# Sigmoid attention followed by a gated FFN on one core: one FFN chunk between the last score units of batch 0, one pair of loads ahead of two weight loads, one DMA transpose sooner

## The chip, the cores and the metric

The kernel runs on one core of one Trainium2 chip. The metric is device microseconds (us) of one execution; the number compared is the median over runs. A profiled execution gives the trace that is read here. Times written like 49.38 are microseconds from the start of that execution's span.

## The reference

Two layers follow each other. `q`, `k` and `v` have 8 batches, 12 heads, 448 rows and head size 64.

```python
scores = q @ k.transpose(0, 1, 3, 2) / np.sqrt(64) - np.log(448)
attn = 1.0 / (1.0 + np.exp(-scores))
x = (attn @ v).transpose(0, 2, 1, 3).reshape(3584, 768)
gate = np.maximum(x @ w_gate, 0.0)        # 768 x 1536
val = x @ w_val                           # 768 x 1536
out = (gate * val) @ w_out                # 1536 x 768
```

The sigmoid has no row sum, so a score block can be turned into attention values as soon as it is computed. All inputs and the output are float32; the kernel computes matmuls in float16 with float32 sums.

## The kernel before

The heads of a batch are worked off in three groups of four heads (`g` = 0 to 2). The scores of a group need its queries and keys transposed: `qkT`. For batches 0 and 1 TensorE does that (`pe_transposes`, L195: fourteen transposes each for keys and queries into a PSUM bank, then one VectorE copy into `qkT`, L206). From batch 2 on, `dma_transposes` (L211) does it: two VectorE copies put keys and queries into a buffer `rel` (L215; two such buffers take turns), and a DMA transpose issued by SyncE writes `qkT` (three buffers).

The steps that follow are:

- A **score unit** multiplies one 64-column chunk of keys with the queries (`qk`, L232, matmuls of 64x64 tiles, four running in the four quarters of the array), and ScalarE writes the sigmoid into `PT` (L187).
- **pv** (L250) multiplies `PT` with the values, and VectorE scales the result into `xT` (L184), the FFN's input.
- An **FFN chunk** (`gv`, L304) is six matmuls with a 128-column block `f` of `w_gate` and six with that of `w_val` (both L309), then a relu and a product into `hT` (L327). The relu is on VectorE (L320) for the first four chunks and on ScalarE (L318) for the next ones. The chunks wait in `gv_queue` in a fixed order, and `ffn_mix(n)` takes n of them.
- The down projection with `w_out` comes later, and from batch 2 on the matmuls use a scheme with fewer products (L393). The change does not touch that part.

The order on every engine is the order in which the program is written out. For batch 0 it is a list of six **slots** (three groups, first 256 queries and then the other 192), each of four units. A dictionary `after` says what follows unit `u` of slot `i`. The slots' score banks are two pairs of PSUM banks used in turn, so a unit waits until the sigmoid of the unit two before has read its pair; four other banks serve transposes, pv and FFN chunks in rotation. Around the change the list reads:

```python
(4, 1): lambda: ffn_then_pv(3),
(4, 3): lambda: ffn_mix(2),
(5, 1): slots[4].pv,
(5, 2): lambda: (pe_transposes(1, 0, 0), pe_transposes(1, 0, 1)),
```

After the last unit comes `slots[5].pv()`, and then batch 1 starts with group 0, whose `qkT` the transposes at (5, 2) make. Batches 1 to 7 run in **bursts** of score units with FFN chunks between them. Batch 1 has six bursts with 4, 3, 3, 3, 3, 4 chunks; `hooks` puts other work between a burst's chunks: an entry `(n, job)` runs when n chunks of that burst are left. `both(1, 1)` and `both(1, 2)` are TensorE transposes of batch 1's second and third group; `dma_transposes(2, 0)`, `(2, 1)` and `late_loads` belong to batch 2. `late_loads` (L741) does `dma_transposes(2, 2)`, then `hold(2, 2)`, a GpSimd copy that waits for that transpose, then the loads of batch 2's values and of `w_out`, in that order on GpSimd's queue.

All loads but the first two are issued by GpSimd into one DMA queue, in the order of the program, as float32 in memory and float16 on the chip. An issue waits until the load eight places before it has landed. `load(b, g0, g1, "kq")` issues keys and then queries of a batch's group (L110, 224 KB each as written), `load_gv(f0, f1)` issues the blocks f0 to f1 - 1 of `w_gate` and then of `w_val` (L148, 576 KB each for three blocks). Twenty FFN chunks of batch 0 run in batch 1; the first that needs block 9 is the first chunk of the fifth burst.

Of the kernel before, what the change touches and what calls it, by code (L numbers as in the profile page):

```python
# [17 lines left out]
def kernel(  # L18
# [62 lines left out]
    def bank16(name):  # L81
        return bank(name, (P, 1024), FP16)
# [11 lines left out]
    def tiles_of(b):  # L94
        if b not in in_tiles:
            pool = early if b == 1 else inp
            in_tiles[b] = tuple(
                p.tile([P, NPAIR, NCH * D], FP16, tag=t, name=t)
                for p, t in ((pool, "k16"), (pool, "q16"), (vinp, "v16"))
            )  # L100
        return in_tiles[b]

    def rows_of(src, b):
        return src[b].rearrange("(x r) (t c) d -> (r t) x (c d)", r=2, c=NCH)

    def load(b, g0, g1, which, c0=0, c1=NCH):
        for nm, t16, src in zip("kq", tiles_of(b), (k, q)):
            if nm in which:
                xs, cs = slice(2 * g0, 2 * g1), slice(c0 * D, c1 * D)
                nc.gpsimd.dma_start(t16[:, xs, cs], rows_of(src, b)[:, xs, cs])  # L110

    def load_v(b):
        v16 = tiles_of(b)[2]
        nc.gpsimd.dma_start(v16[:, 0::2, :], rows_of(v, b)[:, 0::2, :])
        for r in range(2):
            nc.gpsimd.dma_start(
                v16[64 - 64 * r : P - 64 * r, 1::2, :], rows_of(v, b)[64 * r : 64 * r + 64, 1::2, :]
            )
# [25 lines left out]
    def load_gv(f0, f1, which=(0, 1)):  # L144
        fs = slice(f0 * P, f1 * P)
        for i in which:
            wt, src = ((wg, moe_w_gate), (wv, moe_w_val))[i]
            nc.gpsimd.dma_start(wt[:, :, fs], src[:, fs].rearrange("(c p) f -> p c f", p=P))  # L148
# [7 lines left out]
    load_gv(6, 9)  # L156
    load(1, 1, 2, "kq")
    load_v(1)
    load_gv(9, 12)
    load(1, 2, 3, "kq")  # L160

    def load_o():
        for m0, m1 in ((0, 512), (512, DM)):
# [26 lines left out]
    def qkT_of(b, g):  # L190
        if (b, g) not in qkT_tiles:
            qkT_tiles[(b, g)] = qkTp.tile([P, TW, P], FP16, tag="qkT", name="qkT")
        return qkT_tiles[(b, g)]

    def pe_transposes(b, g, ti, c0=0, c1=NCH):  # L195
        t16 = in_tiles[b][ti]
        qkT = qkT_of(b, g)
        trt = bank16("trt")
        for c in range(c0, c1):
            for h in range(2):  # L200
                nc.tensor.transpose(
                    trt[64 * h : 64 * h + 64, c * P : (c + 1) * P],
                    t16[:, 2 * g + h, c * D : (c + 1) * D],
                    ident[:],
                )
        nc.vector.tensor_copy(  # L206
            qkT[:, ti * NCH + c0 : ti * NCH + c1, :].rearrange("p c x -> p (c x)"),
            trt[:, c0 * P : c1 * P],
        )

    def dma_transposes(b, g):  # L211
        k16, q16, _ = in_tiles[b]
        rel = relp.tile([P, TW, P], FP16, tag="rel", name="rel")
        for ti, t16 in enumerate((k16, q16)):
            nc.vector.tensor_copy(  # L215
                rel[:, ti * NCH : (ti + 1) * NCH, :].rearrange("p c (h d) -> p h c d", h=2),
                t16[:, 2 * g : 2 * g + 2, :].rearrange("p h (c d) -> p h c d", c=NCH),
            )
        nc.sync.dma_start_transpose(
            qkT_of(b, g)[:], rel[:].rearrange("p c x -> p (c x)")  # L220
        )
# [437 lines left out]
    def ffn_mix(count, hooks=()):  # L659
        hooks = list(hooks)  # L660
        for left in range(count, -1, -1):
            while hooks and hooks[0][0] >= left:
                hooks.pop(0)[1]()
            if left:
                gv_queue.popleft()()
# [10 lines left out]
    slots = [FirstSlot(half * NG + g, g, half) for half in range(2) for g in range(NG)]  # L676
# [5 lines left out]
    def first_of_second_group():  # L682
        pe_transposes(0, 1, 0, 0, KCUT)
        pe_transposes(0, 1, 1, 0, QCUT)

    def ffn_then_pv(i):
        ffn_mix(1)
        slots[i].pv()
# [16 lines left out]
        (3, 2): second_queries,  # L705
        (3, 3): lambda: ffn_mix(1),
        (4, 1): lambda: ffn_then_pv(3),
        (4, 3): lambda: ffn_mix(2),
        (5, 1): slots[4].pv,
        (5, 2): lambda: (pe_transposes(1, 0, 0), pe_transposes(1, 0, 1)),  # L710
    }
    for i, slot in enumerate(slots):
        for u in range(4):
# [23 lines left out]
    def both(b, g):  # L737
        pe_transposes(b, g, 0)
        pe_transposes(b, g, 1)
# [49 lines left out]
    for b in range(1, B):  # L789
        if b == 1:  # L790
            cuts, pv_at = (0, 3, 6, 9, 13, 17, 21), {3: (0, 2), 5: (1, 2)}
        else:
            cuts, pv_at = (0, 4, 7, 11, 14, 18, 21), {0: (-1, 2), 2: (0, 2), 4: (1, 2)}
        bursts = list(range(len(cuts) - 1))
        inner = {}
        if b > 2:
            inner = {0: 1} if b % 2 == 0 else {2: 3, 3: 5} if b == B - 1 else {4: 5}
            for n in inner.values():
                bursts.remove(n)
        count = len(bursts)  # L800
        hooks = {}
        if b == 1:
            mix = (4, 3, 3, 3, 3, 4)
            hooks = {
                1: [(1, lambda: both(1, 1))],
                3: [(1, lambda: both(1, 2))],
                4: [(3, lambda: dma_transposes(2, 0)), (1, lambda: dma_transposes(2, 1))],
                5: [(3, late_loads)],
            }
        elif b == 2:  # L810
            mix = (2, 2, 1, 1, 1, 2)
            hooks = {
                2: [(0, prepare)],
                4: [(0, lambda: weight_sums(0))],
                5: [(1, lambda: weight_sums(1)), (0, lambda: weight_sums(2))],
            }
            open_late()
        elif b == 3:
            mix = (1, 1, 1, 0, 0)
        else:  # L820
            mix = (0,) * count

        def burst(n):
            for i, (g, c) in enumerate(order[cuts[n] : cuts[n + 1]]):
                if n in pv_at and i == pv_at[n][1]:
                    if n == 0:
                        pv_finish(b - 1)
                        if b == 2:
                            push_group(0)
                        elif b % 2 == 0:  # L830
                            push_group(b // 2 - 1)
                    else:
                        pv_group(b, pv_at[n][0])
                qk_unit(b, g, c)

        if b == 3:
            dma_transposes(3, 2)
            for args in put_off:
                stored(*args)
        for m in range(count):  # L840
            jobs = []
            burst(bursts[m])
            if m == 0 and b > 3:
                jobs.append(lambda: dma_transposes(b, 2))
            if b == 2 and m == count - 1:
                jobs.append(lambda: (dma_transposes(3, 0), dma_transposes(3, 1)))
            elif b == 3 and m == count - 1:
                jobs.append(lambda: dma_transposes(4, 1))
            elif 0 <= m - count + 2 and 3 < b < B - 1:
                jobs.append(lambda: dma_transposes(b + 1, m - count + 2))  # L850
            if b == 1:
                if m == 0:
                    load(2, 0, 1, "kq")
                    load(2, 1, 2, "kq")
                    load(2, 2, 3, "kq")
            elif m == 0 and b + 1 < B:
                if b == 3:
                    jobs.append(lambda: hold(3, 2))
                jobs.append(lambda: (load(b + 1, 0, 3, "kq"), load_v(b + 1)))
            if b % 2 and b > 2:  # L860
                if m == count - 1:
                    jobs.append(lambda: (batch_sums_t1(b // 2), batch_sums(b // 2, (0, 1))))
            elif b > 3 and m == 0:
                jobs.append(lambda: batch_sums(b // 2 - 1, (1, HD)))
            if b == 2 and m == count - 1:
                ffn_mix(mix[m], hooks[m])
                next_work(jobs + [lambda: weight_sums(3)], first_act=True)
            elif mix[m]:
                for job in jobs:
                    job()  # L870
                ffn_mix(mix[m], hooks.get(m, ()))
            else:
                next_work(jobs, amid=(lambda: burst(inner[m])) if m in inner else None)
            if b == 3 and m == count - 2:
                dma_transposes(4, 0)
            if b == 3 and m in (1, 3):
                for f in range(*((0, 8, 2), (8, NFC, 2))[m // 2]):
                    gate_sums(f, f + 2)
# [35 lines left out]
```

## Time and profile before

| what | value |
|---|---|
| median of 3 runs | 394.65 us (394.11 to 394.99) |
| the profiled execution's own time | 393.31 us |
| its span, first to last instruction | 391.5 us |
| TensorE (PE) busy | 384.7 us, 98% |
| VectorE (DVE) / ScalarE (ACT) busy | 282.5 us, 72% / 227.7 us, 58% |
| GpSimd (POOL) busy | 49.4 us, 13% |
| granted TensorE clock | 0.999 |
| the 16 DMA engines, slices 1 to 6 of 40 (the first 59 us) | 9 tenths busy or more |

PE is the row of matmuls and PEld that of weight loads, which run beside them. The ends of matmuls are modelled, so two groups that follow each other overlap in the records; distances between starts are used here instead of durations. An entry in square brackets at the end of a timeline row is the idle time of the engine just before it, and what ended that idle time.

### The profile page before, as it was taken

To read this page: it belongs to the slowest core of one execution; us is meant where nothing else is said; L and a number is where in the kernel's file an instruction comes from. 1 tells how busy PE (TensorE), PEld (TensorE's weight loads), DVE (VectorE), ACT (ScalarE), POOL (GpSimd) and SP (SyncE) were. 2 spreads that over 40 slices of the span, in tenths; PEclk is the share of its full clock that TensorE was granted. 3 is DMA by queue.
4 is the path that set the end of the run, shared out by engine and by line. 5 is a ranking of instruction groups with operands and counts; after the bars stand their busy time and mean duration, and the time that the engine had idled before them with its cause. 6 is when DMAs were issued, how large, how long until landed. Compare 5 with 4: busy or idle time off the path is not lost.

```text
span 391.5 us, 8756 instructions
## 1 busy us (share of the span) xinstructions
PE 384.7 (98%) x3488; PEld 215.8 (55%) x3488; DVE 282.5 (72%) x556; ACT 227.7 (58%) x482; POOL 49.4 (13%) x73
## 2 busy tenths in 40 slices
PE   8999999999999999999999999999999999999995
PEld 3678776445455555454555554545455555555563
DVE  2453344358387789999857779999987788999563
ACT  5957876785777755555556774545467354333322
POOL 9643302500210300003000300000000000000000
PEclk9999999999999999999999999999999999999999
DMA  9999995998999893225956596143002320000335
GB/s 152 199 198 205 203 185 88 198 203 150 198 193 153 156 209 58 47 49 62 173 105 140 111 184 126 20 44 64 18 15 73 78 80 2 0 1 2 79 89 156
DMA packets 68953, 43.69 MB, mean 112 GB/s; under 512 B 35888, under 2 KB 65584, under 8 KB 68912
## 3 DMA queue, kind: packets, MB, share of 16 engines
q0 software_dynamic: 30736, 23.33, 40.1%
q1 hardware_dynamic: 37664, 19.24, 24.5%
q10 hardware_dynamic: 512, 0.56, 0.5%
q8 instruction: 27, 0.44, 0.5%
q14 instruction: 14, 0.11, 0.1%
HBM read 47.19 MB, written 11.01 MB: 149 GB/s over the span
## 4 chain that ended last, share of the span: by engine, by line
PE 85%; DMA 10%; POOL 2%; DVE 1%; issue 1%; ACT 0%; POOLq 0%; DVEq 0%; ACTq 0%
PE u L393 33%; PE g L393 16%; PE y L393 10%; PE qk_ps L232 7%; PE pv_ps L250 6%; PE g_ps L309 5%; PE v_ps L309 5%; DMA k<-in_k_dram 4%; DMA q<-in_q_dram 3%; DMA wg<-in_moe_w_gate_dram 3%; PE ya L354 1%; POOL q L110 1%; PE yb L354 1%; POOL k L110 1%; ACT PT L187 0%
## 5 line engine op out<-in xcount | busy, mean ns | idle before, releaser
L187 ACT ACTIVATE PT<-qk_ps 128x448 f16<-128x448 f32 (+3 forms) x318 | 150.9, 587 | 75.5 <-PE qk_ps L232 75.2
L393 PEld LDWEIGHTS <-S 128*128 128x128 f16 x558 | 54.6, 98 | 44.7
L605 DVE TENSOR_TENSOR gsb<-g,gsb 128x448 f32<-128x448 f32 x72 | 42.8, 624 | 10.1 <-PE g L393 9.8
L232 PE MATMUL qk_ps<-qkT 64*64 64x448 f16 (+2 forms) x756 | 48.0, 336 | 1.0 <-ACT PT L187 0.6
L327 DVE TENSOR_TENSOR hT<-gate_sb,v_ps 128x256 f16<-128x256 f32 (+2 forms) x36 | 16.2, 465 | 36.6 <-ACT gate_sb L318 18.5
L393 PEld LDWEIGHTS <-hT 128*128 128x128 f16 x306 | 28.7, 98 | 22.2 <-issue 4.8
L601 ACT COPY gsb<-u 128x448 f32<-128x448 f32 x48 | 25.6, 558 | 24.0 <-PE u L393 22.9
L445 ACT ACTIVATE ysb<-u 128x384 f32<-128x384 f32 x31 | 15.2, 490 | 38.3 <-PE u L393 33.8
L250 PE MATMUL pv_ps<-PT,v 64*64 64x448 f16 (+2 forms) x756 | 37.1, 329 | 0.2 <-ACT PT L187 0.2
L184 DVE TENSOR_SCALAR xT<-pv_ps 128x448 f16<-128x448 f32 (+2 forms) x53 | 27.9, 567 | 11.8 <-PE pv_ps L250 10.7
L309 PE MATMUL g_ps<-xT,wg 128*128 128x256 f16 (+2 forms) x216 | 33.5, 291 | 0.0
L309 PE MATMUL v_ps<-xT,wv 128*128 128x256 f16 (+2 forms) x216 | 33.3, 290 | 0.0
L393 PEld LDWEIGHTS <-wg 128*128 128x128 f16 x216 | 20.2, 98 | 21.8 <-issue 4.3
L393 PEld LDWEIGHTS <-wv 128*128 128x128 f16 x216 | 21.1, 98 | 19.7
L232 PEld LDWEIGHTS <-qkT 64*64 64x64 f16 x756 | 18.4, 105 | 22.1 <-issue 14.7
L463 DVE SCALAR_TENSOR_TENSOR ysb<-y,ysb 128x384 f32<-128x384 f32 x29 | 16.1, 556 | 17.9 <-PE y L393 10.4
L250 PEld LDWEIGHTS <-v 64*64 64x64 f16 x756 | 22.1, 107 | 10.7 <-issue 1.0
L110 POOL DMA_DIRECT2D k<-in_k_dram x14 | 10.9, 777 | 113.1 <-DVE rel L215 105.6
L393 PE MATMUL u<-T,hT 128*128 128x384 f16 x132 | 25.1, 326 | 0.0
L309 PEld LDWEIGHTS <-wg 128*128 128x128 f16 x216 | 18.7, 98 | 11.4 <-issue 5.2
L309 PEld LDWEIGHTS <-wv 128*128 128x128 f16 x216 | 20.2, 98 | 7.4
L393 PE MATMUL u<-xT,wg 128*128 128x448 f16 x108 | 23.5, 354 | 0.0
(76 smaller groups left out, 532.3 us busy)
## 6 DMA issues: line engine op xcount, KB each, us to landing
out_dram<-ysb SPq DMA_DIRECT2D x52, 192.0 KB, 2.9
k<-in_k_dram POOLq DMA_DIRECT2D x5, 672.0 KB, 11.9
q<-in_q_dram POOLq DMA_DIRECT2D x5, 672.0 KB, 14.9
v<-in_v_dram POOLq DMA_DIRECT2D x8, 336.0 KB, 15.1
v<-in_v_dram POOLq DMA_DIRECT2D x16, 168.0 KB, 15.0
k<-in_k_dram POOLq DMA_DIRECT2D x8, 224.0 KB, 11.8
wo<-in_moe_w_out_dram POOLq DMA_DIRECT2D x1, 1536.0 KB, 13.1
q<-in_q_dram POOLq DMA_DIRECT2D x6, 224.0 KB, 12.2
```

Source lines behind the costliest of these rows:

```text
L110: nc.gpsimd.dma_start(t16[:, xs, cs], rows_of(src, b)[:, xs, cs])
L184: nc.vector.tensor_scalar(out=xT, in0=src, scalar1=XSCALE, scalar2=None, op0=AOP.mult)
L187: nc.scalar.activation(PT_ap, ps_ap, AF.Sigmoid, bias=sig_bias, scale=qk_scale)
L232: nc.tensor.matmul(out_of(hh)[o : o + 64, :], qkT[rows, c, cols], qkT[rows, NCH + c0 : NCH + c1, cols], start=True, stop=True, tile_positi ...
L250: nc.tensor.matmul(ps[hh][64 * r : 64 * r + 64, 0:qn], v16[rows, 2 * g + hh, c * D : (c + 1) * D], pieces[c][rows, hh, :], start=(c == 0), ...
L309: nc.tensor.matmul(ps[-1][:, 0:qn], wt[:, dc, f * P : (f + 1) * P], xT_tiles[b][:, dc, q0 : q0 + qn], start=(dc == 0), stop=(dc == NDC - 1),)
L327: nc.vector.tensor_tensor(out=hT_tiles[g][:, f, o : o + qn], in0=gate_sb[:, 0:qn], in1=ps[1][:, 0:qn], op=AOP.mult,)
L393: nc.tensor.matmul(ps[:, 0:n], A[:, k_, :], W[:, k_, :], start=(first and k_ == 0), stop=(k_ == kn - 1), skip_group_check=True,)
L445: nc.scalar.activation(o, ps[:, 0:HM], AF.Copy, scale=OUT_SCALE)
L463: nc.vector.scalar_tensor_tensor(out=o, in0=ps[:, 0:HM], scalar=OUT_SCALE, in1=o, op0=AOP.mult, op1=AOP.add)
L601: by(gs[u][i][:], ps[u][:, 0:S])
L605: nc.vector.tensor_tensor(out=gs[u][i][:], in0=ps[u][:, 0:S], in1=gs[u][i][:], op=AOP.add)
```

## The change

Three edits. First, one of the two FFN chunks after slot 4's last unit moves behind slot 4's pv, that is, between the second and third unit of slot 5, and the transposes for batch 1's first group move from behind slot 5's third unit to behind its fourth. Second, the load of batch 1's third keys and queries goes ahead of the load of weight blocks 9 to 11. Third, in batch 1's last burst `late_loads` runs ahead of the first FFN chunk instead of behind it.

```diff
@@ -156,8 +156,8 @@
     load_gv(6, 9)
     load(1, 1, 2, "kq")
     load_v(1)
+    load(1, 2, 3, "kq")
     load_gv(9, 12)
-    load(1, 2, 3, "kq")
@@ -683,6 +683,10 @@
+    def pv_then_ffn(i):
+        slots[i].pv()
+        ffn_mix(1)
+
@@ -705,9 +709,9 @@
         (3, 3): lambda: ffn_mix(1),
         (4, 1): lambda: ffn_then_pv(3),
-        (4, 3): lambda: ffn_mix(2),
-        (5, 1): slots[4].pv,
-        (5, 2): lambda: (pe_transposes(1, 0, 0), pe_transposes(1, 0, 1)),
+        (4, 3): lambda: ffn_mix(1),
+        (5, 1): lambda: pv_then_ffn(4),
+        (5, 3): lambda: (pe_transposes(1, 0, 0), pe_transposes(1, 0, 1)),
     }
@@ -805,7 +809,7 @@
                 4: [(3, lambda: dma_transposes(2, 0)), (1, lambda: dma_transposes(2, 1))],
-                5: [(3, late_loads)],
+                5: [(4, late_loads)],
```

No instruction is added or removed. On PE, sixteen score matmuls and pv of slot 4 come one chunk sooner, and the last four score matmuls come ahead of the transposes; on VectorE, two `xT` writes pass a relu and a product, and the two `rel` copies of batch 2's third group pass one product; on GpSimd's queue, two loads pass two others.

## The prediction

> **What bounds the kernel now.** I read the page first, then the chain that ended last, then PE's timeline around the three edits. The page gives the frame:
>
> ```profile
> PE 384.7 (98%) x3488; PEld 215.8 (55%) x3488; DVE 282.5 (72%) x556; ACT 227.7 (58%) x482; POOL 49.4 (13%) x73
> ```
>
> PE is the bound over the whole span, so an edit is worth what it takes out of PE's row. The chain says where PE was last held by something else, in order of time (start, length, what):
>
> ```profile
> 21.97 14.78 DMA k<-in_k_dram
> 36.76 0.29 issue
> 37.05 12.29 DMA q<-in_q_dram
> 49.34 0.04 issue
> 49.38 0.58 PE trt L201 x14
> ```
>
> Up to 49.34 the chain is the load queue, and it enters PE at the transposes of batch 1's third queries. After that it is almost all PE. So what PE loses before 49.38 is not lost to the end unless it pushes past 49.38; conversely, once that load is early, the chain moves to what held PE before it. PE's timeline at the first edit:
>
> ```profile
> 24.47 0.82 PE L309 MATMUL g_ps<-xT,wg 128*128 128x256 f16 x6
> ...
> 25.87 0.53 PE L232 MATMUL qk_ps<-qkT 64*64 64x192 f16 x16
> 26.23 0.75 PE L250 MATMUL pv_ps<-PT,v 64*64 64x192 f16 x28
> 27.20 0.36 PE L232 MATMUL qk_ps<-qkT 64*64 64x192 f16 x8 [0.23 <-ACT PT L187]
> 27.49 0.58 PE L201 MATMUL trt<-ident,k 128*64 128x128 f16 x14
> ...
> 29.33 0.28 PE L250 MATMUL pv_ps<-PT,v 64*64 64x192 f16 x4 [0.16 <-ACT PT L187]
> 29.41 0.76 PE L232 MATMUL qk_ps<-qkT 64*64 64x448 f16 x12
> ```
>
> Slot 5's third unit and the end of its pv wait for sigmoids: ACT idled 1.91 us before 26.34 because two FFN chunks gave it nothing. The same view at batch 1's second and third transposes:
>
> ```profile
> 37.58 0.58 PE L201 MATMUL trt<-ident,k 128*64 128x128 f16 x14
> 38.00 0.56 PE L201 MATMUL trt<-ident,q 128*64 128x128 f16 x14
> 38.49 0.67 PE L309 MATMUL g_ps<-xT,wg 128*128 128x192 f16 x6
> ...
> 48.28 0.58 PE L201 MATMUL trt<-ident,k 128*64 128x128 f16 x14
> 49.38 0.58 PE L201 MATMUL trt<-ident,q 128*64 128x128 f16 x14 [0.52 <-DMA q<-in_q_dram]
> 49.90 0.83 PE L309 MATMUL g_ps<-xT,wg 128*128 128x256 f16 x6
> ```
>
> The same 28 transposes take 0.91 us from start to next work at 37.58 and 1.62 at 48.28. The distances also show the wait that the 0.52 in brackets understates.
>
> **Edit 1, the FFN chunk and the first transposes.** Laid out again from starts. The first chunk begins at 23.15 as now. A chunk and its turn to score matmuls takes 25.87 - 24.47 = 1.40: slot 5's first two units start at 24.55. They take 26.23 - 25.87 = 0.36: pv of slot 4 at 24.91; slot 4's last sigmoid ended at 24.43 (its ACT row, 23.25 + 1.19), so it is ready. pv takes 0.60 (the row 22.20 to 22.80): 25.51. The turn from pv to a chunk is in no row. The nearest is score units to a chunk: twelve matmuls at 22.80 and a chunk at 23.15 are 0.35, of which the matmuls need 0.25, so 0.10; the bounds are 0 and 0.36 (PEld's idle before a chunk at 30.10). I take 0.10, since both are 64x64 tiles giving way to the full array: 25.61. The chunk: 27.01. Twelve score matmuls (0.25) and their turn to the transposes (0.12: 27.20 to 27.49 less 0.17): transposes at 27.38 instead of 27.49. The sigmoids are then not last: ACT reads the first unit from about 25.0 and frees its pair by 25.9.
>
> Next late is VectorE. Transposes starting at 27.49 had their second copy (L206, 28.12 + 1.16) done at 29.28, 1.79 later; batch 1's first scores need that, and PE starts 0.05 after a releasing engine ends (27.15 to 27.20 for ACT). So they start at 27.38 + 1.79 + 0.05 = 29.22 instead of 29.41, although pv of slot 5 is done by 28.29 + 0.60 = 28.89: PE idles 0.33 there. Edit 1 is worth 0.19, not the 0.52 of what PE could do. Its other costs lie beside: the chunk's relu and product (VectorE, 0.42 each) end at about 27.6, before the copies start at 28.0.
>
> Then 0.10 of it is lost again. At 38.00 the second group's queries had landed at 37.9 (issue 23.72, 14.2 us to landing). 0.19 sooner, PE would be there at 37.81 and waits until 37.91, the landing plus the 0.04 seen at 49.34. That load is not moved. What is left of edit 1 after it is **0.09**.
>
> **Edit 2, the loads.** Loads land in one queue with full backlog (DMA 9 tenths throughout), at distances of their size: `w_gate` blocks 9 to 11 at 44.2 (29.96 + 14.2), `w_val` at 47.0 (32.85 + 14.2), keys at 48.2, queries at 49.34. The two weight loads take 5.7 us of the queue, keys and queries 2.3. With the order turned, keys land at about 42.4, queries at 43.6, weights at 46.5 and 49.3. The eight-back wait now holds the weights' issues until about 35.9 and 37.1 instead of 29.96 and 32.85, still 8 us before the queue gets to them. Queries are wanted at 48.7 and have 5 us. The transposes then take 0.91 instead of 1.62: **0.71**. What is late next: the weights' first reader is the chunk at 52.33, then at 51.5, its `w_val` half 0.65 later at 52.2. `w_gate` has 5.0 us of cover, `w_val` 2.9. If that cover were gone, PE would wait for the difference, one for one.
>
> Whether a place in the queue is a place in the landing can be asked of the Trainium skill too. "DMA: Bandwidth & Descriptors", section "Two DMAs through the same engine are not ordered", says that transfers of one queue start in order but are not bound to finish in it. By that alone the sum would lose up to 0.71; the trace shows each of the 35 loads on GpSimd's queue up to 56 us landing in the order of its issue, so I keep it as a rival only.
>
> **Edit 3, the third transpose sooner.** VectorE's two `rel` copies (0.39 each, at 60.62 and 60.92) pass one product. They need the `rel` buffer of `dma_transposes(2, 0)`, whose transpose was issued at 52.61 and took 6.7 us, to 59.3. VectorE gets there at about 58.2 and waits some 1.1 us; behind it stand the products of the last burst. They come out at about 60.1 to 60.5 and 60.5 to 60.9; unhindered they would be at 59.5 and 60.4. Their PSUM banks are wanted by batch 2's first units at 62.91 - 0.80 = 62.1 and 62.3. Cover 1.4 us or more: **0**. The issue on SyncE, the `hold` on GpSimd and the loads behind it start up to 1 us sooner; no PE row after 63 waits for them, so no gain: VectorE's turn could cost, not win. From 49.9 to 63 PE, ACT and VectorE wait on one another at the same distances and move as a block.
>
> **Sum.** 0.09 + 0.71 = 0.80. The profiled execution took 393.31 (span 391.5, 1.8 around it): 392.51. The median of the runs is 1.34 above that execution; I take the difference over: 394.65 - 0.80 = 393.85, 0.20% less. About 0.2%, 0.79 us, is what a measurement of this kernel can tell from no change, so the forecast stands on that line.
>
> **Rivals.**
> - The queries of group 1 land 0.1 or more sooner, or PE runs with more slack to the queue, and edit 1 keeps its 0.19: 0.90, 393.75. For it: 37.9 against 37.81 is a race of a tenth. 0.24, faster.
> - The turn pv to chunk costs its upper bound 0.36: transposes at 27.64, scores at 29.48, 0.07 later than now; 0.64 left, 394.0. Against it: no turn of that kind cost over 0.12. 0.12, same.
> - The queue runs some 0.35 us sooner against PE in ordinary runs than in the profiled one. The present wait is then 0.36 and edit 1 keeps 0.19: 0.55, 394.1. 0.10, same.
> - The change does not do what it says: the pair still lands about when the weights do. Only 0.09 is left, 394.55. Against it: the landings in order. 0.04, same.
> - Slower: VectorE, stuck behind edit 3's copies. It is on PE's path if `dma_transposes(2, 0)` lands after about 60.9 (1.2 us of copies, product and handshake before 62.1). In the profile it shared the engines with the loads until 56.2 and took 6.7 us, the later two 4.0 and 4.2. If it took 11 us from 52.1, PE would wait 2.2 at 62.1: 1.4 slower in all, 396.05. 0.08.
>
> The forecast itself has 0.42, of which 0.26 lies over the line and 0.16 within. So faster 0.26 + 0.24 = 0.50, same 0.16 + 0.12 + 0.10 + 0.04 = 0.42, slower 0.08. The range takes in 0.90 and 0.55 and the scatter of the three runs (0.54 below, 0.34 above their median): 393.3 to 394.5; the last two rivals, 0.12, are left out.
>
> **What would show it.** Right: no bracket of a DMA at the third group's query transposes; scores of batch 1 from about 29.2, with a wait for `qkT` L206 in place of ACT; the chain entering PE at the second group's queries, near 37.9; the fifth burst's first chunk near 51.5 with no DMA wait; VectorE waiting about 1 us for `qkT<-rel` ahead of the third `rel` copies. Wrong: a DMA `wg` or `wv` wait on PE near 52, PE waiting for `hT` L327 near 62, or transposes of the first group starting after 27.5.

## The result, and the profile after

| | kernel before | changed kernel |
|---|---|---|
| median of 11 runs | 394.13 us (393.82 to 394.99) | 393.21 us (392.85 to 394.01) |
| ratio of the two, 95% interval | | 0.9975 [0.9965, 0.9984] |
| the profiled execution and its span | 393.31 us, 391.5 | 393.42 us, 391.6 |

The changed kernel is faster by 0.25%, about 0.98 us of 394.13. The two profiled executions do not show it: before's lies below all its 11 runs and after's above the median of its own. So the spans can't be compared here, and the traces are read stretch by stretch. First the page of the changed kernel, its span, the row of engines and the shares of the chain that ended last:

```profile
span 391.6 us, 8756 instructions
...
PE 385.6 (98%) x3488; PEld 215.7 (55%) x3488; DVE 282.6 (72%) x556; ACT 227.7 (58%) x482; POOL 49.4 (13%) x73
...
PE 96%; ACT 2%; DVE 1%; issue 0%; DVEq 0%; ACTq 0%
```

The same line of the kernel before was:

```profile
PE 85%; DMA 10%; POOL 2%; DVE 1%; issue 1%; ACT 0%; POOLq 0%; DVEq 0%; ACTq 0%
```

The load queue is gone from the chain. The chain of the changed kernel around the place where the loads had entered it (start, length, what):

```profile
48.73 0.49 PE v_ps L309 x6
49.23 0.90 PE trt L201 x28
50.13 0.76 PE g_ps L309 x6
```

PE's timeline at the same place, and then at the first edit. Where before had a bracket with 0.52 of waiting for `q`, there is none now, and the two transposes and the chunk follow at 0.41 and 0.49:

```profile
49.16 0.58 PE L201 MATMUL trt<-ident,k 128*64 128x128 f16 x14
49.57 0.56 PE L201 MATMUL trt<-ident,q 128*64 128x128 f16 x14
50.06 0.83 PE L309 MATMUL g_ps<-xT,wg 128*128 128x256 f16 x6
```

```profile
25.45 0.75 PE L250 MATMUL pv_ps<-PT,v 64*64 64x192 f16 x28
26.13 0.83 PE L309 MATMUL g_ps<-xT,wg 128*128 128x256 f16 x6
26.80 0.82 PE L309 MATMUL v_ps<-xT,wv 128*128 128x256 f16 x6
27.55 0.44 PE L232 MATMUL qk_ps<-qkT 64*64 64x192 f16 x12
27.92 0.58 PE L201 MATMUL trt<-ident,k 128*64 128x128 f16 x14
28.33 0.33 PE L201 MATMUL trt<-ident,q 128*64 128x128 f16 x5
29.13 0.44 PE L201 MATMUL trt<-ident,q 128*64 128x128 f16 x9 [0.47 <-issue]
29.50 0.77 PE L250 MATMUL pv_ps<-PT,v 64*64 64x192 f16 x28
30.29 0.76 PE L232 MATMUL qk_ps<-qkT 64*64 64x448 f16 x12
```

Both waits for sigmoids (ACT `PT` L187, 0.23 and 0.16 before) are gone. In their place the query transposes break off after five of fourteen, and the sixth starts 0.80 after the first, with nothing in the trace that releases it ("issue"). By the records of single matmuls the step from the fifth to the sixth is 0.69, where steps between these transposes are otherwise at most 0.05.

All later comparisons use this table of distances on PE, start to start, from the timelines of one profiled execution each. "All, again" is the changed kernel in a second profiled execution, further below.

| stretch, us | before | after | edit 1 | edit 2 | edit 3 | all, again |
|---|---|---|---|---|---|---|
| span's start to slot 4's chunk | 23.15 | 23.69 | 24.21 | 23.61 | 23.53 | 23.08 |
| to batch 1's first scores | 6.26 | 6.60 | 6.61 | 6.26 | 6.31 | 6.12 |
| to the chunk behind group 1's transposes | 9.08 | 9.08 | 9.08 | 9.08 | 9.34 | 9.14 |
| to the third group's key transposes | 9.79 | 9.79 | 9.79 | 9.79 | 9.82 | 9.80 |
| to the chunk behind them | 1.62 | 0.90 | 1.02 | 0.91 | 1.64 | 0.90 |
| to batch 2's first scores | 13.01 | 13.01 | 13.02 | 13.01 | 13.01 | 13.02 |

After less before is +0.54, +0.34 and -0.72 in the three stretches that differ: +0.16 at batch 2's first scores. The first of the three lies wholly ahead of the change. The 9.34 of edit 3 is in a stretch that edit 3 does not touch: there the second group's queries landed at 38.62 and held PE until 38.66, so that stretch varies wherever PE meets the load queue.

### The profile page after: what moved, and what is told of

The parts are those of the page before. It is cut to its first block, busy times and chain, and to the rows that moved or that the text cites. A ratio compares the mean times of both kernels' runs of the same rounds, so it can differ in the third digit from the quotient of the medians.

```text
span 391.6 us, 8756 instructions
## 1 busy us (share of the span) xinstructions
PE 385.6 (98%) x3488; PEld 215.7 (55%) x3488; DVE 282.6 (72%) x556; ACT 227.7 (58%) x482; POOL 49.4 (13%) x73
## 4 chain that ended last, share of the span: by engine, by line
PE 96%; ACT 2%; DVE 1%; issue 0%; DVEq 0%; ACTq 0%
PE u L393 33%; PE g L393 16%; PE y L393 10%; PE qk_ps L232 9%; PE pv_ps L250 8%; PE g_ps L309 8%; PE v_ps L309 7%; ACT PT L187 2%; PE ya L354 1%; PE warm_ps L175 1%; PE trt L201 1%; PE yb L354 1%; DVE ysb L463 0%; DVE S L384 0%; DVE hT L384 0%
## 5 line engine op out<-in xcount | busy, mean ns | idle before, releaser
L187 ACT ACTIVATE PT<-qk_ps 128x448 f16<-128x448 f32 (+3 forms) x318 | 150.9, 587 | 76.6 <-PE qk_ps L232 76.3
```

The source lines that it names most:

```text
L187: nc.scalar.activation(PT_ap, ps_ap, AF.Sigmoid, bias=sig_bias, scale=qk_scale)
```

## The experiments

The first four kernels ran beside the kernel before in five rounds on one chip; its median there was 394.09 (393.19 to 394.95, 33 runs).

**Edit 1 alone.**

```diff
+    def pv_then_ffn(i):
+        slots[i].pv()
+        ffn_mix(1)
-        (4, 3): lambda: ffn_mix(2),
-        (5, 1): slots[4].pv,
-        (5, 2): lambda: (pe_transposes(1, 0, 0), pe_transposes(1, 0, 1)),
+        (4, 3): lambda: ffn_mix(1),
+        (5, 1): lambda: pv_then_ffn(4),
+        (5, 3): lambda: (pe_transposes(1, 0, 0), pe_transposes(1, 0, 1)),
```

> Edit 1 alone (FFN chunk and first transposes; loads and third DMA transpose as before). Theory of the prediction: batch 1's scores start 0.19 us sooner relative to the chunk after slot 4's first units, but the third group's query transposes still wait for their load, which lands near 49.3 whatever PE does, so the wait grows by what PE gained: time against before 0.0 us (ratio 1.000). Rival, each edit is worth its own part: -0.1 to -0.2 us (0.9995 to 0.9997) and the wait at the third group's queries stays at 0.7 us. A third possibility, VectorE's copies do not hold the scores: -0.5 us.

Measured: 394.29 (393.36 to 394.88, 12 runs), ratio 1.0007 [0.9999, 1.0015]. Edit 1 by itself gains nothing that can be measured. That was expected also if edit 1 works, since the old load order takes its gain back; so this run does not tell whether edit 1 has a worth of its own. Its PE timeline has the same break, after the same five transposes:

```profile
28.45 0.58 PE L201 MATMUL trt<-ident,k 128*64 128x128 f16 x14
28.86 0.33 PE L201 MATMUL trt<-ident,q 128*64 128x128 f16 x5
29.66 0.44 PE L201 MATMUL trt<-ident,q 128*64 128x128 f16 x9 [0.47 <-issue]
```

So the break comes with edit 1 and needs neither the loads nor the last burst. PE came late to the third group in this execution (49.69), so the old load order cost it only 0.12 there (1.02 against 0.90).

**Edit 2 alone.**

```diff
-    load_gv(9, 12)
     load(1, 2, 3, "kq")
+    load_gv(9, 12)
```

> Edit 2 alone (third keys and queries ahead of weight blocks 9 to 11). Theory: the pair lands near 43 to 44, the weights' last half near 49 to 50, no wait for a load on PE after 40; the 28 transposes of the third group take 0.91 us instead of 1.62: -0.71 us (ratio 0.9982), less by as much as PE reaches them later than in the profile of before. Rival, the weights' later landing or the order of landings takes it back: 0.0 us, with a wait of PE for wg or wv near 52.

Measured: 393.13 (392.82 to 394.6, 11 runs), ratio 0.9979 [0.9968, 0.9990]. By itself this is as fast as the whole change within the interval, and its only differing stretch after the start is the third group's: 0.91 instead of 1.62.

**Edit 3 alone.**

```diff
-                5: [(3, late_loads)],
+                5: [(4, late_loads)],
```

> Edit 3 alone (batch 2's third DMA transpose ahead of the last burst's first chunk). Theory: nothing on PE's path moves: 0.0 us (ratio 1.000); VectorE waits up to 0.4 us at the copies for the first transpose's landing and PE shows no wait for VectorE near 63. Rival, VectorE's wait reaches PE: slower by 0.2 us or more, with a wait of score matmuls for the product L327 near 63. Second rival, the loads behind it come sooner and something later gains: faster by over 0.2 us.

Measured: 394.06 (393.8 to 394.53, 11 runs), ratio 1.0004 [0.9995, 1.0012]; from the chunk behind the third transposes to batch 2's first scores 13.01 us as before. Within that interval it is worth nothing and costs nothing. VectorE waited 0.53 for the earlier transpose (up to 0.4 had been expected).

**The changed kernel again,** on the chip of these three.

> The changed kernel once more, beside its parts and on the same chip. Theory: the sum of edits 1 and 2 as they act together, -0.8 to -0.95 us (ratio 0.9976 to 0.9980); more than edit 2 alone by 0.1 to 0.2. If the parts simply add, it is e1 + e2 + e3.

Measured: 392.88 (392.48 to 393.54, 9 runs), ratio 0.9975 [0.9966, 0.9984], the profiled execution 392.48 with a span of 390.7. PE's timeline at the first edit and at the second group:

```profile
27.31 0.58 PE L201 MATMUL trt<-ident,k 128*64 128x128 f16 x14
27.73 0.77 PE L201 MATMUL trt<-ident,q 128*64 128x128 f16 x14
28.42 0.77 PE L250 MATMUL pv_ps<-PT,v 64*64 64x192 f16 x28
29.20 0.76 PE L232 MATMUL qk_ps<-qkT 64*64 64x448 f16 x12
...
37.38 0.58 PE L201 MATMUL trt<-ident,k 128*64 128x128 f16 x14
37.83 0.58 PE L201 MATMUL trt<-ident,q 128*64 128x128 f16 x14
38.34 0.67 PE L309 MATMUL g_ps<-xT,wg 128*128 128x192 f16 x6
```

The query transposes of the first group take 0.69 to the next work instead of 0.49: the same break, 0.21 long this time. The second group's queries, landed at 37.78, let PE start at 37.83, 0.45 after the keys instead of 0.42. The ratios of the three parts multiplied are 0.9990; each of the four intervals is some 0.001 to either side, so that is not told apart from 0.9975. Nor is the whole from edit 2 alone. VectorE in the last burst:

```profile
59.67 0.39 DVE L215 COPY rel<-k 128x896 f16<-128x896 f16 x1 [1.55 <-DMA qkT<-rel]
59.98 0.39 DVE L215 COPY rel<-q 128x896 f16<-128x896 f16 x1
60.28 0.75 DVE L327 TENSOR_TENSOR hT<-gate_sb,v_ps 128x256 f16<-128x256 f32 x2
```

VectorE does wait for the earlier DMA transpose, 1.55 us, and the products come out at 60.7 and 61.0. PE takes no notice: 13.02.

The next kernels ran beside the kernel before in another set (before's median 393.92, 393.31 to 394.77, 21 runs). The first two are tries at a better version: they try to remove, one after the other, what still held PE.

**The second group's keys and queries sooner too.** On top of the change:

```diff
-    load_gv(6, 9)
     load(1, 1, 2, "kq")
+    load_gv(6, 9)
```

> The changed kernel with the load of batch 1's second keys and queries also ahead of a pair of weight loads (blocks 6 to 8). Theory: the second group's queries land near 32 instead of 37.8, so that PE no longer meets them at the transposes near 37.4; 0.03 to 0.1 us sooner than the changed kernel, which these rounds can hardly resolve: ratio to before 0.9972 to 0.9976. In the trace the two transposes of group 1 take 0.91 us together. Rival, the weights now come late: a wait for wg or wv near 40, slower than the changed kernel.

Measured: 393.02 (392.5 to 394.1, 11 runs), ratio 0.9981 [0.9972, 0.9991]. The ratio is above the one that was expected. At the second group the wait is gone (0.42 and 0.48), but that was 0.03 to 0.06 (0.45 against 0.42; 9.14 against 9.08), and at the first group the break was 0.53 long:

```profile
27.69 0.33 PE L201 MATMUL trt<-ident,q 128*64 128x128 f16 x5
28.33 0.44 PE L201 MATMUL trt<-ident,q 128*64 128x128 f16 x9 [0.31 <-issue]
28.70 0.77 PE L250 MATMUL pv_ps<-PT,v 64*64 64x192 f16 x28
```

**The first transposes back at (5, 2),** on top of that kernel, with the chunk still behind slot 4's pv:

```diff
-        (5, 3): lambda: (pe_transposes(1, 0, 0), pe_transposes(1, 0, 1)),
+        (5, 2): lambda: (pe_transposes(1, 0, 0), pe_transposes(1, 0, 1)),
```

> As e5, and batch 1's first transposes stay behind slot 5's third unit (as before the change), while the FFN chunk is between the units. If VectorE's two copies hold batch 1's scores, they now end about 0.1 us sooner relative to the chunk before, and scores start 0.1 us sooner: ratio to before 0.9970 to 0.9975. If PE's instructions hold it (a new block of 256 instructions at PE's instruction 958 is there only about 1.5 us after its fetch), the wait sits at the same count, four matmuls further into the query transposes, and 0.0 to 0.1 us are gained.

Measured: 393.12 (392.83 to 393.63, 11 runs), ratio 0.9977 [0.9968, 0.9986]. No break this time; slot 5's pv waits 0.16 for a sigmoid as it did before:

```profile
27.74 0.58 PE L201 MATMUL trt<-ident,k 128*64 128x128 f16 x14
28.16 0.56 PE L201 MATMUL trt<-ident,q 128*64 128x128 f16 x14
...
29.57 0.28 PE L250 MATMUL pv_ps<-PT,v 64*64 64x192 f16 x4 [0.16 <-ACT PT L187]
```

From slot 4's chunk (23.59) to batch 1's first scores (29.66) it took 6.07, the shortest of all, 0.19 less than before; the time shows no difference from the change itself. Neither try beats the changed kernel.

**What breaks the transposes off.** The break has no releaser in the trace. The DMA records offer one: a queue of instructions.

```profile
q8 instruction: 27, 0.44, 0.5%
```

That is the changed kernel's page (packets, MB, share): 27 packets of 0.44 MB / 27 = 16 KB. PE runs 3488 matmuls and 3488 weight loads, 6976 / 27 = 258 instructions for each packet, so each looks like a block of 256. The places where PE stood still with no releaser in the first 30 us are PE's instructions 446, 702 and 958, that is 256 apart, in every execution that has such a stop. By the trace's records of that queue (packet's start, its end, and PE's start at the next boundary; "stop" is the step from the matmul before):

```
                     boundary      packet              PE goes on   end to PE   PE's stop
after, 446           16.73         14.26 to 15.21      16.73        1.52        0.16
after, 702           22.94         20.49 to 21.43      22.94        1.51        0.15
after, 958           29.13         26.75 to 27.69      29.13        1.44        0.69
edit 1, 446          17.27         14.81 to 15.76      17.27        1.51        0.54
edit 1, 702          23.47         21.01 to 21.95      23.47        1.52        0.14
edit 1, 958          29.66         27.21 to 28.15      29.66        1.51        0.69
all again, 958       28.05         25.60 to 26.56      28.05        1.49        0.21
group 1 early, 958   28.33         25.84 to 26.73      28.33        1.60        0.53
before, 958          28.14         25.59 to 26.48      28.14        1.66        none
edit 2, 958          28.59         26.26 to 27.15      28.59        1.44        none
back at (5, 2), 958  28.38         25.90 to 26.84      28.38        1.54        none
```

PE goes on 1.44 to 1.60 after the packet's end where it stopped. At the boundaries of the first 30 us where it did not stop, it came there 1.65 or more after the packet's end, but for three: 1.44 with edit 2, 1.54 with the transposes back at (5, 2) and 1.57 with edit 3. So the packet's end tells the time of the break to some 0.2, not more closely. In the ten profiled executions the first three packets start 2.9 to 4.0 us after the boundary before was crossed (22.94 to 26.75 in the changed kernel: 3.8) and take 0.9 to 1.0. If that is the cause, a block can't take less here than about 2.9 + 0.9 + 1.4 = 5.2 in the best case and 4.0 + 1.0 + 1.6 = 6.6 in the worst (an estimate from these figures). Before needs 5.74 for the third block; with edit 1 the same instructions would need 0.2 less (5.52 in the second execution, 28.05 less 22.32 less the stop of 0.21) and, when their packet is late, run into it.

The Trainium skill, "Runtime: NRT & Kernel Launch", section "Instruction fetch mechanics", has such blocks: 256 instructions each, fetched by the engine's own queue, the cost of crossing a boundary "mostly hidden". The block's size agrees with the 27 packets; "hidden" does not in this stretch, if the reading above holds. Two kernels, run once each, shift the count of instructions against the work by running the first ten warming matmuls as 22 shorter ones (24 PE instructions more), on the changed kernel and on the kernel before:

```diff
-        for _ in range(count):
-            nc.tensor.matmul(ps[:, 0:S], zeros[:, 0:P], zeros[:], start=True, stop=True)
+        n = 204 if count == 10 else S
+        for _ in range(22 if count == 10 else count):
+            nc.tensor.matmul(ps[:, 0:n], zeros[:, 0:P], zeros[:, 0:n], start=True, stop=True)
```

> The changed kernel with the first ten warming matmuls of 448 columns replaced by 22 of 204: the same time, 24 PE instructions more, everything else the same. Theory (instruction blocks of 256): the stall without a named releaser stays at the same count of matmuls, number 479, which is now twelve matmuls earlier in the work: after the seventh of the fourteen key transposes instead of the fifth query transpose; 0.2 to 0.8 us long. Rival (something of those query transposes, their data or their bank): it stays at the fifth query transpose.

Measured: 392.47, one run, span 390.7. The changed kernel with the shift (its lines are one lower):

```profile
27.31 0.66 PE L202 MATMUL trt<-ident,k 128*64 128x128 f16 x14
27.78 0.58 PE L202 MATMUL trt<-ident,q 128*64 128x128 f16 x14
28.29 0.77 PE L251 MATMUL pv_ps<-PT,v 64*64 64x192 f16 x28
29.22 0.76 PE L233 MATMUL qk_ps<-qkT 64*64 64x448 f16 x12 [0.15 <-DVE qkT L207]
```

Nothing stops in the queries now (0.51); the keys take 0.47 instead of 0.41, and the records put a stop of 0.09 behind the seventh key transpose: twelve matmuls sooner in the work, at the same count of instructions, 1.39 after its packet's end. It is shorter than the 0.2 to 0.8 that had been expected. In this one run the place follows the count, not the work. With the break small, the wait that the prediction named as next shows: batch 1's scores wait for VectorE's second copy. They start 6.15 after slot 4's chunk, no sooner than the 6.12 of the second execution with its break of 0.21: beside VectorE's wait a break that short cost next to nothing, while the two of 0.69 cost about 0.5.

> The kernel before with the same 24 instructions more. Theory of instruction blocks: the kernel before reaches matmul 479 only 0.0 to 0.2 us after its block is there; twelve matmuls earlier it comes up to 0.3 us sooner, so a stall of 0.1 to 0.3 us appears at matmul 479, which it does not show now. Rival: no stall there, as before.

Measured: 393.58, one run, span 391.8. The kernel before with the shift has no stop at that count:

```profile
27.97 0.58 PE L202 MATMUL trt<-ident,k 128*64 128x128 f16 x14
28.39 0.56 PE L202 MATMUL trt<-ident,q 128*64 128x128 f16 x14
```

Its block's packet had ended 1.87 before PE came there, so the stop that I had expected in it was not borne out. So far as these runs go, the place of the break is fixed by a count of 256 instructions; that the packet sets its time is argued from the table and not shown. That the packet is late because the load queue keeps the DMA engines full was not tried either (no kernel took that traffic away). The trace has only a hint: the six packets of the changed kernel that started with no other DMA traffic in the 2 us before, all after 160 us, started 0.7 to 2.4 us ahead of the boundary before, not 3.6 to 3.8 behind it; PE's blocks take 13 to 24 us there, so that is no clean comparison.

## Why the prediction was right, and where it was not

The direction and the mechanism of edit 2, which carries the sum, hold, and 0.80 lies within the measured interval (0.63 to 1.38); edit 1's part of it, 0.09, is not shown. The time given, 393.85, does not hold: 393.21 was measured, below the range's end of 393.3.

**The step that failed is the base.** The prediction worked out 0.80 on one profiled execution, 393.31, and then added 1.34, the distance from that execution to the median of three runs, 394.65. That median was 0.52 too high: with 11 runs before's is 394.13, and the 33 runs beside the parts gave 394.09. From 394.13 the same sum gives 393.33, 0.12 above what was measured. So of the 0.64 between 393.85 and 393.21 the base is 0.52 and the sum 0.12. The range made it worse: its lower end was worked out as a scatter of runs around 394.65, so most of it was used up by the error of that median itself.

On the profile the sum, 392.51, meets the changed kernel's second profiled execution, 392.48, and misses the first, 393.42. Between slot 4's chunk and batch 2's first scores the second gained 0.78 and the first 0.38, because of the longer break; that one of them agrees to 0.03 is in part luck. The chance on "faster by over 0.2%", 0.50, named the case of the measured 0.25%, but the interval, 0.16% to 0.35%, reaches below that line.

**Edit 2, 0.71: right, for a PE as early as in that profile.** The third group's stretch shrank by 0.72 with all edits and 0.71 alone. The landings in the second execution were 42.30 and 43.42 for keys and queries (forecast 42.4 and 43.6), 46.31 and 49.67 for the weights (46.5 and 49.3), in the order of their issue. The rival that transfers of one queue finish out of order fell with that. The queue's eight-back wait put the weights' issues at 35.80 and 36.96 (35.9 and 37.1), and no wait for `wg` or `wv` followed near 52. In the times, too, edit 2 alone carries the change: 0.9979 beside 0.9975, with intervals that overlap. How much the old order costs depends on when PE comes there: in the four profiled executions that have it (before, edit 1, edit 3 and before with the shift) the third group's stretch was 1.62, 1.02, 1.64 and 1.42, so 0.72, 0.12, 0.74 and 0.52 above 0.90.

**Edit 1, 0.19 and then 0.09: the layout right, "next late is VectorE" incomplete.** From slot 4's chunk to the first transposes I had 4.23; it is 4.23 in both executions (23.69 to 27.92, 23.08 to 27.31). The turn from pv to a chunk, guessed at 0.10 between 0 and 0.36, is 0.08 (24.84 to 25.52 is 0.68, of which pv is 0.60). VectorE is next late, as the shifted kernel shows, but a third holder stands beside it that the list of rivals lacked: the break in the query transposes. So batch 1's scores came 0.14 sooner in one execution and 0.34 later in two. The loss of 0.10 at group 1's queries was the right kind and about half the size (0.03 to 0.06), since less was gained ahead of it: 0.08 was left in that one execution, against the 0.09 of the sum. No run shows it in the times. Edit 1 alone (1.0007) was expected at nothing, and the whole beside edit 2 alone (0.9975 and 0.9979) can't resolve a tenth of a microsecond.

**Edit 3, 0: right,** and the mechanism as told: VectorE waited 1.55 (1.1 had been worked out), and the cover behind it held. In the first execution there was no such wait: the copies started at 59.07 and 59.37, after the transpose had landed at 58.66. VectorE was 1.0 later there than in the second execution, and the transpose took 5.9 us instead of 7.3. The slower rival, a transpose landing after 60.9, came in none of them.

The rival of 0.90 with edit 1's gain kept is nearest to the measured 0.92 between medians, but not for its reason: the interval of the ratio, 0.63 to 1.38 us, holds 0.71, 0.80 and 0.90 alike, and in no profiled execution of the changed kernel did edit 1 keep 0.19. The rival in which the queue ran 0.35 sooner against PE was met and passed in one execution, that of edit 1: the queries landed 0.82 later than in before's and PE came 1.41 later, so the old order cost only 0.12.

## What to carry to other kernels

A sum made against one profiled execution should be carried to a base with enough runs: here three of them put the median 0.5 us too high, more than half of the whole effect. Where two kernels differ by less than the start of a run varies, compare start-to-start distances of the same landmarks stretch by stretch: where nothing was changed and PE did not wait for a load they agreed to 0.05 us. And when a wait on the bound engine is removed, look for holders that the waits list can't name before counting the rest as gain: here that was a stop at a fixed count of instructions.

## What the runs showed of the hardware

Short matmuls may outrun their own instructions. Around 25 us PE goes through 256 instructions in 5.5 to 6.2 us, and it stopped at counts that lie 256 apart, by steps of 0.09 to 0.69 us, 1.39 to 1.60 after a 16 KB packet of the instruction queue had ended. The same kernel stopped for 0.69 in one execution and for 0.21 in another.

A good part of the scatter of the runs is made early. From span's start to slot 4's chunk the ten profiled executions took 23.04 to 24.21 us, and already the first scores stood at 6.18 to 6.87; from the third group's chunk to batch 2's first scores all took 13.01 or 13.02. Part of it is PE's first work: eight query transposes at 5.43 took 0.57 in the changed kernel and 0.32 in the kernel before, with the same instructions. The traces show what goes with it. The record of the granted clock starts, at 1.0, at 5.41 us in the kernel before and at 6.56 in the changed kernel, and these transposes follow each other, pair by pair, every 0.106 us ahead of that moment and every 0.055 behind it, which is about twice the pace. Over the ten executions the record starts at 4.20 to 7.00, and the four with the latest starts (6.72 to 7.00) have the latest first scores (6.82 to 6.87). What sets the moment was not tried.
